# Softmax sums as a row through HBM in place of columns: one change to a conformer block on one Trainium2 core

## The chip, the cores and the metric

The kernel runs on one core of a Trainium2 chip. A core has a matmul engine (TensorE, "PE" in the profile; its weight loads are listed apart as "PEld"), a vector engine (VectorE, "DVE"), a scalar engine (ScalarE, "ACT"), GpSimd ("POOL") and a sync engine ("SP") that only issues transfers here. The metric is device time in microseconds (us). "Span" is the time from the first to the last instruction in a profile of one execution. The "granted clock" is the share of TensorE's full clock that the profile shows as granted (1.00 is full, 0.50 half).

## The reference, cut to what matters

The reference is a conformer block in bf16, for 2 batches of 4000 tokens of 512 features: feed-forward, attention, convolution, feed-forward, each with a layer norm and a residual. The change touches the attention:

```python
q = h @ w_q
k = h @ w_k
v = h @ w_v
scores = jnp.einsum('btd,bsd->bts', q, k) * scale
p = _softmax(scores, axis=-1)
attn = jnp.einsum('bts,bsd->btd', p, v) @ w_o
x2 = x1 + attn
```

## The kernel before

The queries are worked on in 16 chunks of 500. For one chunk the kernel goes through 32 tiles of keys. For each tile TensorE computes scores for 128 keys (125 used) by 500 queries, ScalarE takes the exponential into a tile `P`, VectorE adds `P` to a running sum `acc` (keys on the partitions), and four tiles later TensorE multiplies the values with `P` into four banks `Yb` of PSUM (the buffers that TensorE's results go to). The division by the softmax sum comes last, when the output projection is added to the residual: there the sum must lie with queries on the partitions, as `rl` of 125 x 4. When the last values of a chunk are done, this runs:

```python
def finish_queries(self, b, qc, done):
    S, s = self.S, qc % 2
    for dc in range(DC):                      # the output copies: two on VectorE, two on ScalarE
        if dc % 2:
            S.op("DVE", lambda e, dc=dc: e.tensor_copy(self.OT[:, dc, :], self.Yb[dc][:, 0:CHUNK]), ...)
        else:
            self.act(self.OT[:, dc, :], self.Yb[dc][:, 0:CHUNK], AF.Copy, ...)
    S.op("DVE", lambda e: e.tensor_copy(self.ahi, self.acc[s]), ...)              # the splits
    S.op("DVE", lambda e: e.tensor_tensor(out=self.alo, in0=self.acc[s], in1=self.ahi, op=ALU.subtract), ...)

    def sums():
        ps, b_ps = self.sbank()
        for ti in range(TPC):                 # 4 x 2 matmuls of one column
            for part, bp in ((self.ahi, self.b_ahi), (self.alo, self.b_alo)):
                self.mm(ps[0:TILE, ti:ti + 1], part[:, ti * TILE:(ti + 1) * TILE], self.onec[:, 0:1], ...)
        S.op("DVE", lambda e: e.reciprocal(self.rl[s], ps[0:TILE, 0:TPC]), ...)
    ...
    self.after(1 if last else 2, sums)        # so many tiles later
    for ti in range(TPC):
        self.after((2 if last else 4) + ti, lambda ti=ti: project(ti))
```

The comments are added and the read and write lists are cut. The values lag the scores by four tiles, so all this falls into the fourth tile of the next chunk. The program writes down the instructions of each engine in one order; a recording layer puts a semaphore wait (for a signal of another engine) ahead of each instruction that needs one. The scores, the sums and the projections take turns on four PSUM banks. The place between two chunks is called a boundary below. Its cost is the time by which the scores behind it start later than they would if the scores and values of the two chunks followed each other without a gap.

Of the kernel before, what the change touches and what calls it, by code (L numbers as in the profile page):

```python
# [5 lines left out]
F32 = mybir.dt.float32  # L6
BF16 = mybir.dt.bfloat16
I32 = mybir.dt.int32
ALU = mybir.AluOpType
AF = mybir.ActivationFunctionType  # L10
# [3 lines left out]
TILE = 125  # L14
CHUNK = 500
TPC = CHUNK // TILE
# [4 lines left out]
TB = T // TILE  # L21
# [197 lines left out]
class Conformer:  # L219
# [15 lines left out]
    def memory(self):  # L235
        nc = self.nc
# [35 lines left out]
        C = Region(nc, "work", 48992)  # L272
        off = [0]

        def take(n):
            o = off[0]
            off[0] += n
            return o

        oLT = take(2 * 4096)  # L280
# [69 lines left out]
        def small(n, dt=F32, parts=128):  # L350
            return C.view(take(n * (2 if dt == BF16 else 4) + 3 & ~3), n, dt, parts)
# [37 lines left out]
        self.b_one3 = Buf("one3")  # L389
        self.m3 = C.view(oLT + 4096, CHUNK, parts=3)  # L390
        self.b_m3 = [C.buf("m3", oLT + 4096 + j * 250, 250) for j in range(TPC)]
        self.mx = small(TCB, parts=TILE)
        self.b_mx = [Buf("mx") for _ in range(TCB)]
        self.mc = [small(1, parts=TILE) for _ in range(3)]
# [247 lines left out]
    def attention(self, old, hook, done):  # L642
        S = self.S
        LAG = 4
        for g in range(NCK):
            b, qc = divmod(g, TCB)
            s = qc % 2
            if self.any_score:
                if qc == 0:
                    self.pop(len(self.lags))  # L650
                    if b:
                        for kt in range(TB):
                            self.second_keys(kt)
                        for dc in range(DC):
                            self.q_group(1, 0, dc)
                self.row_max(qc)
            for kt in range(TB):
                kc, kj = divmod(kt, TPC)
                ps, b_ps = self.sbank()
                p = self.nxt("P", self.NP)  # L660
                for cc in range(DC):
                    self.mm(ps[:, 0:CHUNK], self.hT[kc][:, kj, cc, :], self.qT[s][:, cc, :],
                            cc == 0, cc == DC - 1 and not self.any_score,
                            [self.b_hT[kc][kj], self.b_qT[s][cc]], b_ps)
                if self.any_score:
                    self.mm(ps[:, 0:CHUNK], self.one3, self.m3, False, True,
                            [self.b_one3] + self.b_m3, b_ps)
                self.act(self.P[p], ps[:, 0:CHUNK], AF.Exp, [b_ps], [self.b_P[p]], scale=SCALE)
                if kt == 0:
                    S.op("DVE", lambda e, p=p: e.tensor_copy(self.acc[s], self.P[p]),  # L670
                         reads=[self.b_P[p]], writes=[self.b_acc[s]])
                else:
                    S.op("DVE", lambda e, p=p: e.tensor_tensor(  # L673
                        out=self.acc[s], in0=self.acc[s], in1=self.P[p], op=ALU.add),
                        reads=[self.b_P[p], self.b_acc[s]], writes=[self.b_acc[s]])

                def values(kt=kt, p=p, b=b, qc=qc):
                    for dc in range(DC):
                        self.mm(self.Yb[dc][:, 0:CHUNK], self.h[kt][:, dc * 128:(dc + 1) * 128], self.P[p],
                                kt == 0, kt == TB - 1, [self.b_h[kt], self.b_P[p]], self.b_Y[dc],  # L680
                                inc=kt == TB - 1 or dc == DC - 1)
                    if kt == TB - 1:
                        self.finish_queries(b, qc, done)

                self.lags.append(values)
                if g == 0 and kt < LAG:
                    self.pop({0: old // 2, 1: old - old // 2}.get(kt, 0))
                elif len(self.lags) > LAG:
                    self.pop(1)
                if g + 1 < NCK and kt in (14, 16, 18, 20) and not (self.any_score and g + 1 == TCB):  # L690
                    self.q_group((g + 1) // TCB, (g + 1) % TCB, (kt - 14) // 2)
                if not self.any_score:
                    if g == TCB - 1 and kt >= 6:
                        self.second_keys(kt - 6)
                    if g == TCB and kt < 6:
                        self.second_keys(TB - 6 + kt)
                hook(g, kt)
                self.tick()

    def second_keys(self, kt):  # L700
# [3 lines left out]
        self.load(self.h[kt], src, [self.b_h[kt]], reads=[self.b_keys2[kc]])  # L704
        self.transpose(self.hT[kc][:, kj], src, [self.b_keys2[kc]], [self.b_hT[kc][kj]])

    def finish_queries(self, b, qc, done):
        S, s = self.S, qc % 2
        for dc in range(DC):
            if dc % 2:  # L710
                S.op("DVE", lambda e, dc=dc: e.tensor_copy(self.OT[:, dc, :], self.Yb[dc][:, 0:CHUNK]),  # L711
                     reads=[self.b_Y[dc]], writes=[self.b_OT[dc]])
            else:
                self.act(self.OT[:, dc, :], self.Yb[dc][:, 0:CHUNK], AF.Copy, [self.b_Y[dc]], [self.b_OT[dc]])
        S.op("DVE", lambda e: e.tensor_copy(self.ahi, self.acc[s]), reads=[self.b_acc[s]], writes=[self.b_ahi])  # L715
        S.op("DVE", lambda e: e.tensor_tensor(out=self.alo, in0=self.acc[s], in1=self.ahi, op=ALU.subtract),  # L716
             reads=[self.b_acc[s], self.b_ahi], writes=[self.b_alo])

        def sums():
            ps, b_ps = self.sbank()  # L720
            for ti in range(TPC):
                for part, bp in ((self.ahi, self.b_ahi), (self.alo, self.b_alo)):
                    self.mm(ps[0:TILE, ti:ti + 1], part[:, ti * TILE:(ti + 1) * TILE], self.onec[:, 0:1],
                            part is self.ahi, part is self.alo, [bp, self.b_onec], b_ps,
                            inc=part is self.alo and ti == TPC - 1)
            S.op("DVE", lambda e: e.reciprocal(self.rl[s], ps[0:TILE, 0:TPC]),
                 reads=[b_ps], writes=[self.b_rl[s]])

        def project(ti):
            ps, b_ps = self.sbank()  # L730
            for dc in range(DC):
                self.mm(ps[0:TILE, :], self.OT[:, dc, ti * TILE:(ti + 1) * TILE], self.Wvo[:, dc, :],
                        dc == 0, dc == DC - 1, [self.b_OT[dc], self.b_Wvo], b_ps)
            self.residual(ps[0:TILE, :], b_ps, (b * TCB + qc) * TPC + ti, self.rl[s][:, ti:ti + 1],
                          [self.b_rl[s]])
            if ti == TPC - 1:
                done(b * TCB + qc)

        last = b * TCB + qc == NCK - 1
        self.after(1 if last else 2, sums)  # L740
        for ti in range(TPC):
            self.after((2 if last else 4) + ti, lambda ti=ti: project(ti))


    def conv_b(self, t, jj):
# [405 lines left out]
```

## Time and profile before

| | before |
|---|---|
| time, median of 3 runs | 2134.14 us (2133.32 to 2136.76) |
| span of the profiled run | 2132.2 us |
| busy: PE, DVE, ACT | 97%, 51%, 34% |
| share of the chain that ended last: PE, DVE | 93%, 3% |
| period of one chunk in attention | 69.42 us |

The chain is followed back from the last instruction; an engine's share in it is the part of the span in which the end waited for that engine. The period is the distance between the first one-column matmuls of two neighbouring chunks; in the trace 13 of the 15 distances are within 0.01 us of 69.42 (the first and the last chunk do less work beside attention). The lines themselves are shown in the prediction.

### The profile page before, as it was taken

What the parts mean: (1) busy time and instruction counts of PE and PEld (TensorE: products, weight loads), DVE (VectorE), ACT (ScalarE), POOL (GpSimd) and SP (SyncE); (2) the same over time, 40 slices, a digit from 0 to 9 for tenths busy, and PEclk for the clock granted to TensorE, in tenths of its full rate; (3) what the DMA queues carried; (4) which work ended last, traced back from release to release, by engine and by line L of the source; (5) the groups of instructions that cost most, each with busy time, mean ns of one, the idle gap of its engine ahead of it and who ended that gap; (6) DMA issues with size and microseconds to landing.
All of it is one profiled execution on the core that took longest, in us unless ns stands there. A gap on an engine that the chain in (4) does not pass through costs nothing.

```text
span 2132.2 us, 24365 instructions
## 1 busy us (share of the span) xinstructions
PE 2058.9 (97%) x9674; PEld 1038.7 (49%) x9674; DVE 1090.5 (51%) x2229; ACT 732.7 (34%) x1248; POOL 122.9 (6%) x257
## 2 busy tenths in 40 slices
PE   4999999999999999999999999999987999999996
PEld 2555555554444444444444444444444555555553
DVE  2444433335555666656665666566745434444442
ACT  1433333333333333333333333333324433443332
POOL 0111100000000000000000000000000000000000
PEclk9999999999999999999999999999999999999998
DMA  7122222110000000004300000000233011111110
GB/s 177 34 56 59 59 60 59 49 49 11 11 5 13 18 15 20 8 18 114 80 10 18 15 18 13 15 18 16 59 107 99 21 38 35 35 30 40 40 38 23
DMA packets 199327, 85.39 MB, mean 40 GB/s; under 512 B 147873, under 2 KB 198692, under 8 KB 199204
## 3 DMA queue, kind: packets, MB, share of 16 engines
q1 hardware_dynamic: 186468, 75.35, 14.6%
q10 hardware_dynamic: 12736, 8.39, 1.5%
q8 instruction: 78, 1.28, 0.3%
q14 instruction: 45, 0.37, 0.1%
HBM read 29.53 MB, written 19.04 MB: 23 GB/s over the span
## 4 chain that ended last, share of the span: by engine, by line
PE 93%; DVE 3%; issue 1%; DMA 1%; ACT 0%; SPq 0%; POOL 0%; ACTq 0%; POOLq 0%; DVEq 0%
PE s L453 53%; PE y L453 39%; DVE work L711 1%; DVE work L716 1%; DVE work L673 0%; DMA xt<-in_x_dram 0%; ACT work L457 0%; DVE work L491 0%; SPq L465 0%; DMA work<-work 0%; DVE work L715 0%; DVE work L514 0%; POOL work L501 0%; DVE xt L560 0%; ACTq L461 0%
## 5 line engine op out<-in xcount | busy, mean ns | idle before, releaser
L457 ACT ACTIVATE work<-s 128x500 bf16<-128x500 f32 (+1 forms) x1068 | 626.8, 587 | 1266.6 <-PE s L453 1262.0
L453 PE MATMUL s<-work,wff 128*128 128x500 bf16 x2560 | 634.3, 378 | 32.2 <-DMA work<-work 28.8
L453 PE MATMUL y<-work,keys 128*128 128x500 bf16 x2048 | 519.1, 374 | 1.3
L453 PE MATMUL s<-work,keys 128*128 128x500 bf16 x2048 | 517.5, 374 | 0.1
L453 PE MATMUL y<-wff,work 128*125 128x512 bf16 x2048 | 514.8, 379 | 0.0
L673 DVE TENSOR_TENSOR work<-work 128x500 f32<-128x500 f32 x496 | 334.8, 675 | 304.6 <-ACT work L457 302.9
L453 PEld LDWEIGHTS s<-work,wff 128*128 128x128 bf16 x2560 | 251.1, 98 | 313.3 <-issue 33.7
L453 PEld LDWEIGHTS y<-wff,work 128*125 128x125 bf16 x2048 | 279.6, 137 | 176.4
L453 PEld LDWEIGHTS y<-work,keys 128*128 128x128 bf16 x2048 | 198.0, 97 | 244.4 <-DVE work L711 15.6
L453 PEld LDWEIGHTS s<-work,keys 128*128 128x128 bf16 x2048 | 199.2, 98 | 228.9 <-DVE work L602 0.6
L560 DVE SCALAR_TENSOR_TENSOR xt<-y,xt 125x512 bf16<-125x512 f32 x128 | 79.4, 683 | 385.5 <-PE y L453 385.5
L491 DVE BATCH_NORM_STATS2 work<-xt 125x6 f32<-125x512 bf16 x320 | 201.6, 679 | 16.8 <-DMA xt<-in_x_dram 16.8
L453 PE MATMUL s<-work 128*125 128x512 bf16 (+2 forms) x646 | 144.8, 347 | 20.8 <-DVE work L716 7.9
L501 POOL TENSOR_TENSOR work<-work 125x4 f32<-125x4 f32 x80 | 85.5, 1068 | 1189.2 <-DVE work L499 1189.2
L514 DVE TENSOR_SCALAR work<-xt,work 125x512 bf16<-125x512 bf16 x288 | 116.0, 449 | 20.1 <-POOL work L501 20.1
L453 PEld LDWEIGHTS s<-work 128*125 128x125 bf16 (+1 forms) x646 | 81.1, 139 | 72.1 <-issue 10.8
L560 DVE SCALAR_TENSOR_TENSOR xt<-s,xt 125x512 bf16<-125x512 f32 x64 | 43.8, 691 | 134.4 <-PE s L453 134.4
L755 DVE SCALAR_TENSOR_TENSOR wff<-wff,s 128x500 bf16<-128x500 f32 x64 | 43.2, 676 | 63.7 <-PE s L453 63.7
L457 ACT ACTIVATE wff<-s 128x500 f32<-128x500 f32 x64 | 37.6, 587 | 81.3 <-PE s L453 76.8
L560 DVE SCALAR_TENSOR_TENSOR xt<-s,work,xt 125x512 bf16<-125x512 f32 x64 | 48.0, 750 | 34.0 <-PE s L453 33.1
L453 PE MATMUL s<-keys,work 128*128 128x500 bf16 x256 | 64.4, 376 | 0.0
L457 ACT ACTIVATE work<-keys,work 128x500 bf16<-128x500 bf16 x64 | 49.6, 794 | 5.9 <-DMA wff<-in_w_ff_a_dram 4.0
(51 smaller groups left out, 397.7 us busy)
## 6 DMA issues: line engine op xcount, KB each, us to landing
xt<-in_x_dram SPq DMA_DIRECT2D x15, 500.0 KB
out_dram<-work SPq DMA_DIRECT2D x15, 500.0 KB
dcvd<-wff SPq DMA_DIRECT2D x52, 125.0 KB, 1.7
keys<-dcvd SPq DMA_DIRECT2D x13, 500.0 KB
wff<-in_w_ff_a_dram ACTq DMA_DIRECT2D x16, 256.0 KB
keys<-work SPq DMA_DIRECT2D x8, 512.0 KB, 3.5
keys<-keys SPq DMA_DIRECT2D x32, 128.0 KB
work<-work SPq DMA_TRANSPOSE x192, 2.5
```

The source lines that it names most:

```text
L453: self.S.op("PE", lambda e: e.matmul(out, lhsT, rhs, start=start, stop=stop), reads=reads, writes=[bank], inc=stop if inc is None else inc)
L457: return self.S.op("ACT", lambda e: e.activation(out, in_, func, **kw), reads=reads, writes=writes)
L491: self.S.op("DVE", lambda e: e.bn_stats(self.st[sl][:, ti, :], self.XT[g]), reads=[self.bx[g]], writes=[self.b_st[sl][ti]])
L501: S.op("POOL", lambda e: e.tensor_tensor(out=self.rs[sl], in0=self.va[sl], in1=self.neghalf[0:TILE, :], op=ALU.pow), reads=[self.b_va[sl], ...
L514: self.S.op("DVE", lambda e: e.tensor_scalar(out, self.XT[g], self.mv[sl][:, ti, 0:1], self.rs[sl][:, ti:ti + 1], ALU.subtract, ALU.mult), ...
L560: self.S.op("DVE", lambda e: e.scalar_tensor_tensor(out=self.XT[g], in0=ps, scalar=scalar, in1=self.XT[g], op0=ALU.mult, op1=ALU.add), rea ...
L673: S.op("DVE", lambda e, p=p: e.tensor_tensor(out=self.acc[s], in0=self.acc[s], in1=self.P[p], op=ALU.add), reads=[self.b_P[p], self.b_acc[ ...
L711: S.op("DVE", lambda e, dc=dc: e.tensor_copy(self.OT[:, dc, :], self.Yb[dc][:, 0:CHUNK]), reads=[self.b_Y[dc]], writes=[self.b_OT[dc]])
L716: S.op("DVE", lambda e: e.tensor_tensor(out=self.alo, in0=self.acc[s], in1=self.ahi, op=ALU.subtract), reads=[self.b_acc[s], self.b_ahi], ...
L755: self.S.op("DVE", lambda e: e.scalar_tensor_tensor(out=self.G[gs][:, jj, 1:1 + CHUNK], in0=self.th[k], scalar=1.0, in1=ps[:, 0:CHUNK], op ...
```

## The change

The intent is to have fewer matmuls on TensorE: two 500-column matmuls with a ones column as weights give all 500 sums as one row. The row lies on one partition, so it is stored to HBM (the memory outside the core) and loaded back with the queries on the partitions. The splits move to the last score tile, and the projections come two tiles later. The last chunk keeps the columns.

```diff
+                if kt == TB - 1:
+                    self.split_sums(s)
...
-        S.op("DVE", lambda e: e.tensor_copy(self.ahi, self.acc[s]), ...)
-        S.op("DVE", lambda e: e.tensor_tensor(out=self.alo, in0=self.acc[s], in1=self.ahi, op=ALU.subtract), ...)
+        def sum_row():
+            ps, b_ps = self.sbank()
+            for part, bp in ((self.ahi, self.b_ahi), (self.alo, self.b_alo)):
+                self.mm(ps[0:1, 0:CHUNK], self.onec[:, 0:1], part, part is self.ahi, part is self.alo,
+                        [bp, self.b_onec], b_ps)
+            self.act(self.row, ps[0:1, 0:CHUNK], AF.Copy, [b_ps], [self.b_row])
+            self.store(self.rowd[s:s + 1, :], self.row, [self.b_row], [self.b_rowd[s]])
+            k = S.dsems[self.nxt("ld", 12)]
+            S.dma("SP", k, lambda e: e.dma_start(self.sq[s], self.rowd[s].rearrange("(t p) -> p t", p=TILE),
+                                                 allow_slow_non_contiguous=True), ...)
...
-        self.after(1 if last else 2, sums)
+        if last:
+            self.after(1, sums)
+        else:
+            sum_row()
+            self.after(5, lambda: S.op("DVE", lambda e: e.reciprocal(self.rl[s], self.sq[s]), ...))
         for ti in range(TPC):
-            self.after((2 if last else 4) + ti, lambda ti=ti: project(ti))
+            self.after((2 if last else 6) + ti, lambda ti=ti: project(ti))
```

The new buffers and the two moved lines inside `split_sums` are cut.

More of the change, by code (lines that the diff above doesn't have):

```diff
@@ L391, in memory @@
         self.b_m3 = [C.buf("m3", oLT + 4096 + j * 250, 250) for j in range(TPC)]
+        self.row = C.view(oLT + 6144, CHUNK, F32, parts=1)
+        self.b_row = C.buf("row", oLT + 6144, 2000)
+        self.sq = [small(TPC, parts=TILE) for _ in range(2)]
+        self.b_sq = [Buf("sq") for _ in range(2)]
+        self.rowd = nc.dram_tensor("rowd", [2, CHUNK], F32, kind="Internal").ap()
+        self.b_rowd = [Buf("rowd") for _ in range(2)]
         self.mx = small(TCB, parts=TILE)
@@ L705, in second_keys, with split_sums @@
         self.transpose(self.hT[kc][:, kj], src, [self.b_keys2[kc]], [self.b_hT[kc][kj]])
+    def split_sums(self, s):
+        S = self.S
+        S.op("DVE", lambda e: e.tensor_copy(self.ahi, self.acc[s]), reads=[self.b_acc[s]], writes=[self.b_ahi])
+        S.op("DVE", lambda e: e.tensor_tensor(out=self.alo, in0=self.acc[s], in1=self.ahi, op=ALU.subtract),
+             reads=[self.b_acc[s], self.b_ahi], writes=[self.b_alo])
     def finish_queries(self, b, qc, done):
@@ L714, in finish_queries @@
                 self.act(self.OT[:, dc, :], self.Yb[dc][:, 0:CHUNK], AF.Copy, [self.b_Y[dc]], [self.b_OT[dc]])
-        S.op("DVE", lambda e: e.tensor_copy(self.ahi, self.acc[s]), reads=[self.b_acc[s]], writes=[self.b_ahi])
-        S.op("DVE", lambda e: e.tensor_tensor(out=self.alo, in0=self.acc[s], in1=self.ahi, op=ALU.subtract),
-             reads=[self.b_acc[s], self.b_ahi], writes=[self.b_alo])
+        def sum_row():
[7 more added lines that the diff above has]
+            S.dma("SP", k, lambda e: e.dma_start(self.sq[s], self.rowd[s].rearrange("(t p) -> p t", p=TILE),
+                                                 allow_slow_non_contiguous=True),
+                  reads=[self.b_rowd[s]], writes=[self.b_sq[s]])
         def sums():
@@ L739, in finish_queries @@
         last = b * TCB + qc == NCK - 1
-        self.after(1 if last else 2, sums)
+        if last:
+            self.after(1, sums)
+        else:
+            sum_row()
+            self.after(5, lambda: S.op("DVE", lambda e: e.reciprocal(self.rl[s], self.sq[s]),
+                                       reads=[self.b_sq[s]], writes=[self.b_rl[s]]))
         for ti in range(TPC):
-            self.after((2 if last else 4) + ti, lambda ti=ti: project(ti))
+            self.after((2 if last else 6) + ti, lambda ti=ti: project(ti))
     def conv_b(self, t, jj):
```

## The prediction

> **What bounds the kernel now.** I read the page in this order: the busy table, the granted clock, the chain, then single chunk boundaries in the timeline of each engine.
>
> ```profile
> PE 2058.9 (97%) x9674; PEld 1038.7 (49%) x9674; DVE 1090.5 (51%) x2229; ACT 732.7 (34%) x1248; POOL 122.9 (6%) x257
> ...
> PE 93%; DVE 3%; issue 1%; DMA 1%; ACT 0%; SPq 0%; POOL 0%; ACTq 0%; POOLq 0%; DVEq 0%
> PE s L453 53%; PE y L453 39%; DVE work L711 1%; DVE work L716 1%; DVE work L673 0%; DMA xt<-in_x_dram 0%; ACT work L457 0%; DVE work L491 0%; SPq L465 0%; DMA work<-work 0%; DVE work L715 0%; DVE work L514 0%; POOL work L501 0%; DVE xt L560 0%; ACTq L461 0%
> ```
>
> TensorE (PE) carries the end; VectorE (DVE) and ScalarE (ACT) are half idle or more. Only what removes TensorE instructions or TensorE waits is worth anything. The chain names the lines the change touches: L711 copies the attention output out of PSUM, L715 and L716 split the softmax sums into a high and a low bf16 part. Together they are a little over 1% of the span. They recur once per query chunk, of which there are 16. Here is one boundary on TensorE (columns: start us, length us, operation, count, idle before it and its releaser):
>
> ```profile
> 609.30 1.00 PE L453 MATMUL y<-work,keys 128*128 128x500 bf16 x4
> 610.14 1.01 PE L453 MATMUL s<-work,keys 128*128 128x500 bf16 x4
> 610.99 1.42 PE L453 MATMUL y<-work,keys 128*128 128x500 bf16 x4
> 612.36 0.22 PE L453 MATMUL s<-work 128*125 128x1 bf16 x1
> 613.07 0.56 PE L453 MATMUL s<-work 128*125 128x1 bf16 x7 [0.49 <-DVE work L716]
> 613.49 1.01 PE L453 MATMUL s<-work,keys 128*128 128x500 bf16 x4
> ```
>
> The first row is the last value product of the old chunk. Then come scores, the first value product of the new chunk, the eight one-column matmuls, and scores again. In steady state four 500-column matmuls advance TensorE by 0.845 us (609.30 to 610.14, 610.14 to 610.99), so the scores at 613.49 would start at 610.14 + 2 x 0.845 = 611.83 with nothing between. The boundary costs 1.66 us, in three parts: the value product is stretched by 612.36 - 611.83 = 0.53; the first one-column matmul and the wait behind it take 613.07 - 612.36 = 0.71; the other seven take 613.49 - 613.07 = 0.42, or 60 ns each. I read the same timeline at all fifteen inner boundaries: fourteen cost 1.66 within 0.01, the first 1.72. The reasons are in the weight loads and in VectorE:
>
> ```profile
> 611.44 0.11 PEld L453 LDWEIGHTS y<-work,keys 128*128 128x128 bf16 x2 [0.56 <-DVE work L711]
> 612.03 0.10 PEld L453 LDWEIGHTS y<-work,keys 128*128 128x128 bf16 x1 [0.47 <-DVE work L711]
> ...
> 610.12 0.68 DVE L673 TENSOR_TENSOR work<-work 128x500 f32<-128x500 f32 x1 [1.01 <-ACT work L457]
> 610.72 1.26 DVE L711 CAST work<-y 128x500 bf16<-128x500 f32 x2
> 611.89 0.41 DVE L715 CAST work<-work 128x500 bf16<-128x500 f32 x1
> 612.34 0.68 DVE L716 TENSOR_TENSOR work<-work 128x500 bf16<-128x500 f32 x1
> ```
>
> VectorE does a running sum, two output copies, then both splits, back to back, and TensorE waits for each in turn. But the split input was ready four score tiles earlier: the values lag the scores by four tiles.
>
> The sixteenth boundary is worse:
>
> ```profile
> 1571.01 1.01 PE L453 MATMUL y<-work,keys 128*128 128x500 bf16 x4
> 1573.52 0.22 PE L453 MATMUL s<-work 128*125 128x1 bf16 x1 [1.50 <-DVE work L715]
> 1574.23 0.91 PE L453 MATMUL s<-work 128*125 128x1 bf16 x7 [0.50 <-DVE work L716]
> 1575.00 1.83 PE L453 MATMUL s<-work,wff 128*128 128x500 bf16 x4
> 1576.62 4.12 PE L453 MATMUL s<-work 128*125 128x512 bf16 x16
> ```
>
> **What the Trainium skill says.** "TensorE: Matmul & The Clock Gate", Back-to-back issue gap: a warm matmul takes N/2.4 + 2.5 ns and below 64 columns there is a floor of about 60 cycles. For 500 columns that is 211 ns; the trace has 0.845/4 = 211, so it agrees. For one column the trace has 60 ns, above the floor's 25: each here also loads a 125-column weight. "DMA: Bandwidth & Descriptors", Anatomy of one DMA: about 2.0 us fixed per transfer. The trace agrees nearly: a 125 KB store to HBM lands in 1.7 us (median of 52). Same page, Rules for kernel authors: a non-contiguous last dimension "lowers to one descriptor per element". The new load writes 125 partitions x 4 separate floats, so 500 pieces of 4 bytes. Same page, Why a DMA increments its semaphore by 16 and not by 1: the number of engines is the largest up to 16 that divides the slowest dimension, so 5 for 125, or 100 pieces each. Nothing in the trace of before shows such a load.
>
> **The change part by part.** (1) *Splits moved* from the end of the values to just after the last score tile's sum. VectorE does the same 0.41 + 0.68 us, four tiles earlier, where a tile lasts 1.69 us and the running sum takes 0.68 of it. The splits no longer stand in the boundary; the 0.49 us wait on L716 and the one on L715 should vanish. (2) *Eight one-column matmuls removed* at 15 boundaries: with (1) they and their waits were 0.71 + 0.42 = 1.13 us. (3) *Two 500-column matmuls added* with the ones column as weights, at once after the last values: 2 x 0.211 = 0.42 us. They stand before the scores, so they also delay the first value product by 0.42, and VectorE gets that time for its copies: the stretch of 0.53 shrinks to about 0.11. New boundary: 0.42 + 0.11 = 0.53. Saved: 1.66 - 0.53 = 1.13 us, times 15 = 17.0 us (17.1 with the costlier first).
>
> (4) *The last boundary* keeps its eight matmuls, but its splits are done long before. TensorE can begin them at about 1572.0 in place of 1573.5, and ends them 0.5 later; one group of four matmuls follows, then the projections, which need the copies (at the latest 1573.14 in the chain). So the projections may start near 1573.4 to 1574 in place of 1576.62. In before the group from 1575.00 takes 1.62 us for four matmuls, twice the usual, so TensorE seems slow after its wait; I can't tell whether this stays. The chain runs through here into the last chunk's normalization. I take 3 us, out of 2 to 4.
>
> (5) *Round trip through HBM*, 15 times. One ACT copy of the 1x500 row, which I estimate at the 587 ns that 128x500 copies take, behind the two output copies: done some 1.8 us after the last values. Store 1.7 us plus 0.3 of issue; then the load: 0.6 issue, 2 fixed, and 100 pieces per engine at 26 ns (the share of queue 1, 14.6% of 16 x 2132 us over 186468 packets, gives 27 ns) makes 2.7. Estimated arrival: about 9 us after the last values. The reciprocal is queued on VectorE behind the running sum of the fifth tile iteration, nominally about 7.7 us (9.4 with convolution work in between) after the values. So VectorE may stand for a microsecond. That costs TensorE nothing: the projections come one tile later, and the first stall could come only when the third projection needs the bank of the first, at about 15 us. Nothing at the end of the span: the last chunk uses no round trip.
>
> (6) *Projections, and the normalization behind them, two tiles (about 4 us) later.* Their transposes end near tile 20; the convolution reads them at tile 22. Free.
>
> Sum: 17 + 3 = 20 us; 2134.1 - 20 = 2114 us, 0.9% less.
>
> **The rivals.** *The output copies bind.* If VectorE is later than I think (its 1.09 us of splits now falls beside the convolution taps' work of tiles 29 to 31), the value product keeps its whole 0.53: saved 0.71 x 15 + 2 = 13 us, so 2121. For: the same engine ends both waits. Against: the splits are four tiles away, and the waits of VectorE on ACT (0.7 to 1.4 us before most running sums) show room. *The round trip binds.* If a 4-byte piece costs 100 ns or more in place of 26, the load takes 13 us; the reciprocal then holds the VectorE queue, and with it residuals, banks and TensorE: a few us in 15 chunks, so 2125 to 2180. Against: the slack of 15 us. *The Sync queue blocks.* It now waits for the row, then for its store, and other transfers stand behind. Beside it run second-batch keys from 963 to 1036 us, back to back; the row of the eighth chunk queues there. For: the queue is full. Against: it is one chunk, and those keys are read about 24 tiles later. Costs 0 to 5 us once. *Only the matmul count matters*: 8 x 60 ns out, 422 ns in, that is nothing: 2133. Against: the waits are in the chain.
>
> **Range and chances.** 2109 if the last boundary gives 4 and the value stretch vanishes (1.24 x 15 = 18.6) and a little more; 2121 from the first rival. Two percent faster would be 2091, more than every wait at every boundary together (16 x 1.7 = 27 would only reach 2107): 1%. Slower by 2% needs the second rival in full: 2%. Within: 97%.
>
> **What would show it.** Right: 9584 matmuls (9674 - 90); no wait of TensorE on the split lines at inner boundaries; a chunk period 1.13 us shorter than the 69.4 us of before (617.04 to 686.46); a value product of about 1.1 in place of 1.42 us; a row load landing in under 6 us. Wrong: VectorE idle for many us before the reciprocal, TensorE waiting for residuals or transposes at tiles 8 to 22, or a value product as long as before.

## The result, and the profile after

The changed kernel took 2118.46 us (median of 4 runs, 2117.57 to 2120.55) beside 2133.73 us of the kernel before (median with a fourth run). The ratio is 0.9927, with a 95% interval of 0.991 to 0.9945. Ratios here are the mean time of one kernel's fast runs over that of the other's of the same rounds, so not quite the ratio of the medians. The gain is 15.3 us by the medians, or about 15.6 by the ratio; the prediction was 20, and 2118.46 lies within its range of 2109 to 2121.

The busy table and the chain of the changed kernel:

```profile
PE 2050.4 (97%) x9582; PEld 1032.4 (49%) x9584; DVE 1090.0 (52%) x2229; ACT 739.3 (35%) x1263; POOL 118.7 (6%) x257
...
PE 95%; issue 1%; DVE 1%; DMA 1%; SPq 0%; POOL 0%; ACT 0%; POOLq 0%; ACTq 0%; DVEq 0%
```

There are 9584 weight loads, 90 fewer, as predicted (two matmul records are missing from the trace). VectorE's share of the chain fell from 3% to 1%. VectorE's work is unchanged, so only its place has changed. The same boundary as in the prediction, TensorE and then its weight loads, in the timeline of the changed kernel (the line numbers of the kernels differ; L453 and L460 are the helper that issues every matmul):

```profile
607.72 1.00 PE L460 MATMUL y<-work,keys 128*128 128x500 bf16 x4
608.66 0.58 PE L460 MATMUL s<-work 128*1 128x500 bf16 x2
609.17 1.02 PE L460 MATMUL s<-work,keys 128*128 128x500 bf16 x4
610.03 1.00 PE L460 MATMUL y<-work,keys 128*128 128x500 bf16 x4
610.87 1.01 PE L460 MATMUL s<-work,keys 128*128 128x500 bf16 x4
...
608.66 0.09 PEld L460 LDWEIGHTS s<-work 128*1 128x1 bf16 x2 [0.41 <-ACT work L464]
609.17 0.54 PEld L460 LDWEIGHTS s<-work,keys 128*128 128x128 bf16 x4 [0.43 <-issue]
```

Without anything between, the scores at 610.87 would start 3 x 0.845 us after 607.72, at 610.255. The boundary costs 0.61 us in place of 1.66, and the chunk period is 68.38 in place of 69.42. The value product is not stretched at all (1.00, from 1.42). The row matmuls themselves cost more than their 0.42: they start 0.10 us after the values could have ended (608.66 against 608.565), and the scores come 0.51 after them. In both places the weight load begins together with its matmul, where weight loads elsewhere begin 0.2 us ahead.

On VectorE the splits are gone from behind the copies, and the reciprocal comes 9.7 us after the last values (618.22 - 608.565) without a wait of its own:

```profile
609.14 1.26 DVE L728 CAST work<-y 128x500 bf16<-128x500 f32 x2
...
618.22 0.17 DVE L770 RECIPROCAL work<-work 125x4 f32<-125x4 f32 x1
```

The round trip on the sync engine's queue, of the same boundary:

```profile
609.93 0.23 SPq L476 DMA_DIRECT2D rowd<-work  x1
611.06 0.25 SPq L741 DMA_DIRECT2D work<-rowd  x1
```

The load is issued when the store has landed, so the store took 1.13 us from issue. The load's pieces moved from 611.94 to 612.67. VectorE never waits for a transfer in the attention stage of this trace. The last boundary of the changed kernel:

```profile
1554.90 1.01 PE L460 MATMUL y<-work,keys 128*128 128x500 bf16 x4
1555.74 0.57 PE L460 MATMUL s<-work 128*125 128x1 bf16 x8
...
1557.02 3.62 PE L460 MATMUL s<-work 128*125 128x512 bf16 x16
```

The projections start 2.12 us after the last value product's start, where it was 5.61 (1571.01 to 1576.62). Both waits of this boundary are gone.

### The profile page after: what moved, and what is told of

It is laid out like the page before. It is cut to its first block, busy times and chain, and to the rows that moved or that the text cites. A ratio compares the mean times of both kernels' runs of the same rounds, so it can differ in the third digit from the quotient of the medians.

```text
span 2113.7 us, 24196 instructions
## 1 busy us (share of the span) xinstructions
PE 2050.4 (97%) x9582; PEld 1032.4 (49%) x9584; DVE 1090.0 (52%) x2229; ACT 739.3 (35%) x1263; POOL 118.7 (6%) x257
## 4 chain that ended last, share of the span: by engine, by line
PE 95%; issue 1%; DVE 1%; DMA 1%; SPq 0%; POOL 0%; ACT 0%; POOLq 0%; ACTq 0%; DVEq 0%
PE s L460 54%; PE y L460 41%; DMA xt<-in_x_dram 0%; DVE work L498 0%; SPq L472 0%; DMA work<-work 0%; DVE work L521 0%; POOL work L508 0%; DVE xt L567 0%; DMA wff<-in_w_ff_b_dram 0%; DMA wff<-in_w_ff_a_dram 0%; DVE wff L851 0%; DVE wff L786 0%; DVE work L504 0%; SPq L468 0%
## 5 line engine op out<-in xcount | busy, mean ns | idle before, releaser
L464 ACT ACTIVATE work<-s 128x500 bf16<-128x500 f32 (+1 forms) x1083 | 635.3, 587 | 1244.0 <-PE s L460 1242.7
L460 PE MATMUL s<-work,wff 128*128 128x500 bf16 x2560 | 630.9, 377 | 32.3 <-DMA work<-work 28.9
L460 PE MATMUL s<-work,keys 128*128 128x500 bf16 x2048 | 517.6, 374 | 0.1
L460 PE MATMUL y<-wff,work 128*125 128x512 bf16 x2048 | 514.8, 379 | 0.0
L460 PE MATMUL y<-work,keys 128*128 128x500 bf16 x2048 | 514.0, 373 | 0.0
L460 PEld LDWEIGHTS s<-work,wff 128*128 128x128 bf16 x2560 | 250.8, 98 | 313.3 <-issue 32.5
L460 PEld LDWEIGHTS y<-wff,work 128*125 128x125 bf16 x2048 | 279.6, 137 | 176.4
L460 PEld LDWEIGHTS y<-work,keys 128*128 128x128 bf16 x2048 | 199.2, 97 | 234.0 <-DVE xt L567 0.2
L460 PEld LDWEIGHTS s<-work,keys 128*128 128x128 bf16 x2048 | 198.6, 98 | 234.9 <-issue 6.0
L460 PE MATMUL s<-work 128*125 128x512 bf16 (+2 forms) x556 | 140.7, 377 | 12.2 <-ACT work L464 8.8
L508 POOL TENSOR_TENSOR work<-work 125x4 f32<-125x4 f32 x80 | 81.1, 1014 | 1240.0 <-DVE work L506 1240.0
L460 PEld LDWEIGHTS s<-work 128*125 128x125 bf16 (+1 forms) x556 | 72.5, 134 | 64.1 <-ACT work L464 11.5
L460 PE MATMUL s<-keys,work 128*128 128x500 bf16 x256 | 64.4, 376 | 0.0
L567 DVE SCALAR_TENSOR_TENSOR xt<-s,work,xt 125x512 bf16<-125x512 f32 x64 | 47.9, 749 | 16.0 <-PE s L460 15.7
```

The source lines that it names most:

```text
L460: self.S.op("PE", lambda e: e.matmul(out, lhsT, rhs, start=start, stop=stop), reads=reads, writes=[bank], inc=stop if inc is None else inc)
L464: return self.S.op("ACT", lambda e: e.activation(out, in_, func, **kw), reads=reads, writes=writes)
L508: S.op("POOL", lambda e: e.tensor_tensor(out=self.rs[sl], in0=self.va[sl], in1=self.neghalf[0:TILE, :], op=ALU.pow), reads=[self.b_va[sl], ...
L567: self.S.op("DVE", lambda e: e.scalar_tensor_tensor(out=self.XT[g], in0=ps, scalar=scalar, in1=self.XT[g], op0=ALU.mult, op1=ALU.add), rea ...
```

## The experiments

The first question was which part of the change gains. Theory M says it is the moved splits; rival R says it is the row.

**split_only**: the kernel before, with the splits moved.

```diff
+                if kt == TB - 1:
+                    self.split_sums(s)
...
-        S.op("DVE", ... self.ahi ...)      # in finish_queries
-        S.op("DVE", ... self.alo ...)
```

> The kernel before with one part of the change: the two splits moved to the last score tile; the eight one-column matmuls stay where they were, after the first value product of the new chunk. Theory M (the gain is the moved splits; the row and HBM only replace cheap matmuls): a boundary loses the waits for the splits but keeps the value product stretched by 0.53 us and pays 8 x 60 ns = 0.48, so about 1.0 in place of 1.66 us: 0.65 x 15 = 10 us, plus 4 us at the last boundary, less some 2 us that the stretch after attention gave back in the changed kernel: 12 us, ratio 0.9945. Rival R (the row and its way round are the gain): nothing at the inner boundaries, 2 us at the last: 0.999.

Measured: 2121.43 us, ratio 0.9934 (0.9922 to 0.9946), chunk period 68.61. The move alone is most of the gain: 0.81 of the 1.04 us of the period, and 0.66 of the 0.73% of the time. It did better than expected; TensorE at the boundary shows why:

```profile
607.74 1.01 PE L453 MATMUL s<-work,keys 128*128 128x500 bf16 x4
608.59 1.42 PE L453 MATMUL y<-work,keys 128*128 128x500 bf16 x4
609.85 0.57 PE L453 MATMUL s<-work 128*125 128x1 bf16 x8
610.28 1.01 PE L453 MATMUL s<-work,keys 128*128 128x500 bf16 x4
```

The boundary is 610.28 - 607.74 - 1.69 = 0.85: 0.43 for the eight columns and 0.42 for the stretch, where I had read 0.53. The other 0.11 in the kernel before was the start of the first one-column matmul, which waited for a split.

**cols_at_once**: the columns also issued at once after the values.

```diff
-        self.after(1 if last else 2, sums)
+        if last:
+            self.after(1, sums)
+        else:
+            sums()
```

> As split_only, and the eight one-column matmuls issued at once after the last values, where the changed kernel issues its row; no row, no HBM, projections where they were. Theory M: the eight matmuls (0.48 us) fill the time that the value product would wait for the copies, so a boundary costs 0.53 to 0.61 us, as with the row (0.61): as fast as the changed kernel or up to 1 us faster, ratio to before 0.992 to 0.993. Rival R: clearly slower than the changed kernel, 0.997 or more.

Measured: 2112.07 us, ratio 0.989 (0.9874 to 0.9906), period 68.20. This kernel has neither row nor HBM and beats the changed kernel, by more than expected. Its boundary:

```profile
606.73 1.01 PE L453 MATMUL y<-work,keys 128*128 128x500 bf16 x4
607.57 0.57 PE L453 MATMUL s<-work 128*125 128x1 bf16 x8
608.00 1.01 PE L453 MATMUL s<-work,keys 128*128 128x500 bf16 x4
608.85 1.00 PE L453 MATMUL y<-work,keys 128*128 128x500 bf16 x4
```

Eight one-column matmuls take 0.43 us (607.57 to 608.00), as much as two of 500 columns should. They hold the value product back by that time, so that VectorE's running sum and copies get far enough ahead, and the product comes unstretched. There is no gap ahead of the columns or behind them. Of the 6.4 us between the medians of the two kernels the boundaries are 2.7 (0.18 x 15); 1.2 is time outside the span, and 1.9 lies behind attention (46.91 us in this profile against 48.84), both taken up below.

**row_only**: the changed kernel with the splits back in their old place, and the row two tiles later.

```diff
-                if kt == TB - 1:
-                    self.split_sums(s)
...
+        self.split_sums(s)                 # behind the output copies
...
-            sum_row()
+            self.after(2, sum_row)
```

> The changed kernel with the splits back behind the output copies, and the two row matmuls two tiles later, where the columns were; round trip, reciprocal and projections as changed. Theory M: the waits for the splits are back (0.53 stretch, 0.71 for the first matmul with its wait), and the second row matmul takes 0.21 in place of 0.42: a boundary of about 1.5 us, last boundary as before: gain 0 to 3 us, ratio 0.9985 to 1.000. Rival R: it keeps most of the gain, 0.994.

Measured: 2134.53 us, ratio 0.9999 (0.9986 to 1.0012), period 69.31. The wait for the split is back:

```profile
612.35 0.37 PE L460 MATMUL s<-work 128*1 128x500 bf16 x1 [0.34 <-DVE work L718]
```

The row and the round trip by themselves gain 0.1 us a chunk, which the time does not show. Rival R falls.

**before_again**: the kernel before, unchanged.

> The kernel before once more, against itself: ratio 1.000 within 0.001. It is run for the relation between time and span: the changed kernel gained 18.5 us of span in the two profiles but 15.3 us of time between medians. If the span of a usual run of before is near 2129.5 (its profiled run was 2.3 us slower than the median), the two agree and nothing is lost outside the span; if it is 2132 with a time of 2133.5, the changed kernel loses about 3 us outside its span.

Measured: 2135.34 us, ratio 0.9999. Five of its six runs lay between 2133.19 and 2137.21, and one at 2138.49; the spans went from 2129.2 to 2134.7. The profiled run that the prediction was made from was thus at the slow end. Time minus span was 3.7 to 4.1 us in all runs of before, against 4.85 to 5.07 in the four of the changed kernel.

The second question was what the row's extra 0.19 us is, and whether the round trip is as far off the path as predicted.

**after_again**: the changed kernel, unchanged.

> The changed kernel once more. Its ratio should be 0.9927 within 0.001. Two things about it are open: its time lay 5.0 us above its span in all four runs, that of the six other kernels' runs 3.7 to 4.1; if this comes from the kernel, 5.0 returns here, if from the chip or the launch, 3.9 and a ratio near 0.992. And TensorE waited 8.8 us for ScalarE near the last weight loads, against 7.4 to 7.9 in the kernels with columns at every boundary; row_only, which has rows, had 8.9: if the rows cause it, 8.8 again.

Measured: 2120.16 us, ratio 0.9926; time minus span 4.7 to 5.4 us. So the extra 1.2 us outside the span belongs to the kernel. The wait of TensorE for ScalarE was 8.7 us again; but later profiles of kernels with columns had 8.2 (cols_again) and 8.4 (hi_copies_first), and ones128 with rows had 7.7, so the rows do not explain it.

**one_wait**: both row matmuls declared to need both splits.

```diff
-                        [bp, self.b_onec], b_ps)
+                        [self.b_ahi, self.b_alo, self.b_onec], b_ps)
```

> The changed kernel with both row matmuls declared to need both splits, so that the second needs no wait of its own. In the changed kernel a boundary costs 0.61 us where two 500-column matmuls are 0.42; TensorE starts the row 0.10 late and the scores 0.09 late. Theory W (the semaphore waits keep the weight loads from being issued ahead): part of the 0.19 goes, boundary 0.52 or less, 1.4 us faster in all. Rival C (loading weights of one column does not overlap with the matmul before and after it): 0.61 as before. For C: the columns at once have the same waits and no such gap.

Measured: 2118.83 us, ratio 0.9927, period 68.38. Nothing changed, so theory W gets no support. It isn't refuted by this run alone: only the second matmul lost its wait, the first kept one. The next run keeps both.

**ones128**: ones in 128 columns as the weights.

```diff
-                self.mm(ps[0:1, 0:CHUNK], self.onec[:, 0:1], part, ...)
+                self.mm(ps[:, 0:CHUNK], self.ones, part, ...)       # ones: 128 x 128, rows 0 to 124 are 1
```

> The changed kernel with a ones matrix of 128 columns as the row's weights in place of one column (all 128 output rows are then the same sum; row 0 is used). Same waits. Theory W: boundary 0.61, as in the changed kernel. Rival C: the weights load ahead like all others and the boundary is 0.42 to 0.45, some 2.7 us faster in all, ratio about 0.9915.

Measured: 2114.59 us, ratio 0.9907 (0.9892 to 0.9922), period 68.19. TensorE and the weight loads:

```profile
607.80 0.58 PE L462 MATMUL s<-work 128*128 128x500 bf16 x2
608.23 1.01 PE L462 MATMUL s<-work,keys 128*128 128x500 bf16 x4
...
607.60 0.31 PEld L462 LDWEIGHTS s<-work 128*128 128x128 bf16 x2
```

The weight loads run ahead again by 0.2 us, and the boundary is 0.43. More weights are faster than fewer: the gap came with the one-column weights. Both waits are still there, so theory W falls. So does the wait for ScalarE that the profile names before the row's weights in the changed kernel: here they load at 607.60, before the last exponential ends at 607.75. That confirms rival C as to the cause being the weights (with them go the rows of the result, 1 against 128, which can't be changed apart); why one column does not load ahead is not shown.

**hops3**: three more round trips ahead of the last.

```diff
-            self.store(self.rowd[s:s + 1, :], self.row, [self.b_row], [self.b_rowd[s]])
+            for hop in range(4):
+                self.store(self.rowd[s:s + 1, :], self.row, [self.b_row], [self.b_rowd[s]])
+                if hop < 3:
+                    self.load(self.row, self.rowd[s:s + 1, :], [self.b_row], reads=[self.b_rowd[s]])
```

> The changed kernel with three more round trips through HBM ahead of the last (row stored, loaded back, stored again). The changed kernel's load had its packets done about 4.5 us after the last values, and the reciprocal came on VectorE at 9.7 us. A hop should take 2.5 to 3.5 us, so the sums arrive at 12 to 15 us. My theory that the round trip lies off the path with some 15 us of room: VectorE now waits a few us at the reciprocal, TensorE does not, time as the changed kernel within 1 us. Rival (any wait of VectorE passes on to TensorE): 2 to 5 us at each of 15 boundaries, 30 to 75 us slower.

Measured: 2115.91 us, ratio 0.992. VectorE waited 39.8 us in all at the 15 reciprocals (6.5 at most), TensorE 1.6 us at one boundary. The reciprocal at the boundary shown above:

```profile
619.57 0.18 DVE L773 RECIPROCAL work<-work 125x4 f32<-125x4 f32 x1 [2.32 <-DMA work<-rowd]
```

A wait of VectorE of this length, in this place, is free. This kernel is even some us faster than after_again of the same chip; 1.2 of that is time outside the span (3.8 us here), and the rest is within the scatter of single spans (2111.6 to 2115.0 here, 2110.8 to 2116.1 there).

**hops6**: the same with six (`range(7)`, `hop < 6`).

> As hops3, with six more round trips. hops3 showed 2.6 us a hop and the reciprocal 12.05 us after the last values, with VectorE waiting 2.3 us and TensorE not. Six put the reciprocal at 12.05 + 7.8 = 19.9 us after the values. By my account TensorE's first stall comes where the third projection needs the bank of the first, 15.9 us after the values; the first residual would then be done at about 21.3, so TensorE stalls some 5.5 us at each of 15 boundaries: 80 us slower than the changed kernel (40 to 110), ratio 1.03. Rival (the room is larger, or the stall is made up): within 10 us of the changed kernel.

Measured: 2229.46 us, ratio 1.0449 (1.0431 to 1.0467), some 110 us slower than the changed kernel, at the upper end of what was expected. TensorE and VectorE at the same boundary:

```profile
637.79 1.97 PE L460 MATMUL s<-work 128*125 128x512 bf16 x4 [5.17 <-DVE xt L567]
...
636.31 0.18 DVE L773 RECIPROCAL work<-work 125x4 f32<-125x4 f32 x1 [10.00 <-DMA work<-rowd]
```

The matmuls at 637.79 are the third projection: the stall is where the prediction put it, and of the size expected (5.17 against 5.5). TensorE waited 83.4 us for residuals in all, 3.4 of them in a place behind attention where before waits as well, so 80 at the boundaries, as expected. The rest is a second cost that I had left out: after the wait the granted clock was 0.50 for 3.3 us (637.79 to 641.10), so eight matmuls took twice their time, some 1.7 us at this stall. Over all 15 stalls the clock records show 68 us at 0.50, which costs up to 34 us.

The third question was whether a better version is to be had.

**cols_hi_only**: cols_at_once with the sums from the high part alone, so four matmuls and one split.

```diff
-        S.op("DVE", ... self.alo ...)
...
-                for part, bp in ((self.ahi, self.b_ahi), (self.alo, self.b_alo)):
-                    self.mm(ps[0:TILE, ti:ti + 1], part[:, ti * TILE:(ti + 1) * TILE], self.onec[:, 0:1], ...)
+                self.mm(ps[0:TILE, ti:ti + 1], self.ahi[:, ti * TILE:(ti + 1) * TILE], self.onec[:, 0:1], ...)
```

> cols_at_once with the sums taken from the high bf16 part alone: four one-column matmuls in place of eight, no second split. It gives slightly less exact denominators (one bf16 rounding per partition, averaged over 125 partitions). With four matmuls between the values and the scores VectorE's copies have 0.22 us less time. If the value product needs the 0.53 us I took from before, the boundary stays at 0.43 or so and nothing is gained; if the copies have room, the boundary falls towards 0.22, up to 3 us faster than cols_at_once, ratio 0.9877.

Measured: 2115.17 us, ratio 0.9912 (0.9896 to 0.9929), period 68.18, correct. The columns now take 0.20 us, but the value product is stretched again:

```profile
606.29 1.00 PE L453 MATMUL y<-work,keys 128*128 128x500 bf16 x4
...
608.18 1.22 PE L453 MATMUL y<-work,keys 128*128 128x500 bf16 x4
609.25 1.01 PE L453 MATMUL s<-work,keys 128*128 128x500 bf16 x4
...
608.43 0.11 PEld L453 LDWEIGHTS y<-work,keys 128*128 128x128 bf16 x2 [0.36 <-DVE work L718]
...
607.11 0.68 DVE L673 TENSOR_TENSOR work<-work 128x500 f32<-128x500 f32 x1 [1.01 <-ACT work L457]
607.71 1.25 DVE L718 CAST work<-y 128x500 bf16<-128x500 f32 x2
```

The boundary is 609.25 - 606.29 - 3 x 0.845 = 0.42. The product's weights wait for the copies (L718), so 0.42 us is a floor as long as VectorE's work stands in this order: running sum, then copies.

**hi_copies_first**: the same, with the running sum of the fourth tile issued behind the output copies.

```diff
+                late = g > 0 and kt == LAG - 1
+                if not late:
+                    add()                  # the running sum of this tile, as before
...
                 elif len(self.lags) > LAG:
                     self.pop(1)            # here the copies are issued
+                if late:
+                    add()
```

> cols_hi_only with VectorE's output copies issued ahead of the running sum of the fourth tile, which stood before them. cols_hi_only showed a boundary of 0.42 us in place of cols_at_once's 0.43: what four matmuls saved, the value product waited for the copies (1.22 us in place of 1.00). If the copies are the floor, taking 0.6 us from in front of them lets the boundary fall to the four matmuls, 0.20 to 0.25 us: 3 us faster than cols_at_once. If something else holds it, 0.42 as before.

Measured: 2110.87 us, ratio 0.9889 (0.9873 to 0.9906), period 67.96. The floor was the running sum in front of the copies: they now start at 607.43, right behind the values, and the sum comes after them. The boundary is 609.54 - 606.81 - 2.535 = 0.20:

```profile
606.81 1.00 PE L453 MATMUL y<-work,keys 128*128 128x500 bf16 x4
...
609.54 1.01 PE L453 MATMUL s<-work,keys 128*128 128x500 bf16 x4
...
607.43 1.26 DVE L725 CAST work<-y 128x500 bf16<-128x500 f32 x2 [0.81 <-PE y L453]
```

The period says 0.24 x 15 = 3.6 us less than cols_at_once. The medians of the shared rounds differ by 1.5 us (2112.40 for cols_again) and the intervals overlap, so the time alone does not prove it; the period does for the stage.

**cols_again**: cols_at_once, unchanged.

> cols_at_once once more, as the yardstick on the same chip and for its spread: its first four runs lay within 0.8 us, those of every other kernel spread over 3 to 5. Ratio 0.989 to 0.991.

Measured: 2112.40 us (2111.38 to 2114.86), ratio 0.9899 (0.9882 to 0.9915). The lead over the changed kernel holds; the narrow spread of its first runs was luck.

## Why the prediction was right, and where its terms were off

Its main reading holds: the waits for the splits were the gain, the round trip is hidden, and TensorE was the only thing to count. The runs confirm each of these apart (split_only 0.9934, row_only 0.9999, hops3 0.992). The sum was 4 to 5 us too good, from several terms. One reading of the chain was off without harm: L711, L715 and L716 are 0.9%, 0.3% and 0.5% of it, so 1.7% and not "a little over 1%".

1. *Splits moved.* Right. There is no wait of TensorE on the split lines in the changed kernel.
2. *Eight matmuls and their waits out, 1.13 us.* Right in the sum, but the split into parts was misread: the stretch is 0.42, and 0.11 of "0.53" belonged to the first one-column matmul.
3. *Two matmuls in, 0.42, plus 0.11 of stretch.* The step is mis-sized. No stretch remained, but the one-column weights cost 0.19 of gaps, so 0.61 in place of 0.53 (ones128: 0.43). Over 15 boundaries the gain was 1.04 to 1.05, so 15.7 us in place of 17.1.
4. *Last boundary, 3 us out of 2 to 4.* Right, as far as two profiles can tell. From the last run of 16 value products to the end of the projections the changed kernel took 10.64 us (1549.83 to 1560.47). Before took 14.64 (1565.94 to 1580.58) and in the repeat 13.02, so the gain was 2.4 to 4.0. The difference between the two runs of before is the clock: in the first it was 0.50 from 1574.2 to 1576.6, after a wait, which is the slowness that the prediction noted and could not place.
5. *Round trip.* Right that it is free, too pessimistic in its size: the load's pieces had moved by about 4.1 us after the values, not 9. The pieces took 9 ns each and not 26 (507 packets from 610.0 to 612.9 made 9.8% of 16 engines' 2.9 us). Of the 507 two belong to the store; the load's 505 are the predicted 500 and five more, one for each engine if five took part, as predicted (the profile doesn't tell the engines apart). The 2.0 us was misapplied: the page's section, "Anatomy of one DMA — SWDGE (gpsimd) path", is about transfers that GpSimd issues, and these are issued by the sync engine. Here the load's first piece moved 0.88 us after its issue and the last was done after 1.61. The limit was as worked out: hops3 below it, hops6 above it, with the stall at the third projection.
6. *Projections later.* Right. No wait for them or for the transposes appears.

Two losses were not in the sum at all. Time outside the span grew by 1.2 us: 5.0 in the changed kernel, one_wait and ones128, and 3.7 to 4.1 in all others, row_only and hops3 among them. It follows the kernel and not the chip, but what makes it stays open. And the stretch behind attention gave some back. From the end of the last projections to the second group of 32 matmuls of the next stage, the changed kernel took 48.84 us and in the repeat 48.36, before 46.83 and 47.34. In the changed kernel 4.3 us of this ran at a granted clock of 0.55 (1569.3 to 1573.6) and the 1.86 us ahead of it at 0.50, behind a wait of 3.40 us that before has too. "TensorE: Matmul & The Clock Gate", What's actually happening, says that the clock halves after an idle window of about 3.4 us and that the window runs freely. The traces fit the free-running window: in the clock records of all runs each stretch between two changes is a whole number of 3.41 us, and with the same 3.40 us wait cols_at_once still had 0.96 just behind it and 0.50 only from 1.1 us later. But the window need not be idle throughout: in before the clock halved at 1574.2 after 3.41 us in which TensorE had been busy for 1.44. So the phase has a part in what a wait costs: behind the same 3.40 us wait the clock stayed at 0.50 for 5.7 us in the changed kernel and for 2.7 in its repeat. This explains the first profile of the changed kernel only; the 48.36 of the repeat has another cause, which stays open. hops3, with the same rows, took 46.36 us for the stretch; so I don't count this as caused by the change.

15.7 for the boundaries, about 3 for the last, less 1.2 outside and 1 to 2 behind attention, makes 15.5 to 16.5; the ratio says 15.6. That is no close check, since the last boundary and the stretch behind attention each vary by 1 to 2 us from profile to profile.

Of the rivals, "the output copies bind" was half right: with the running sum in front of them they do set a floor, at 0.42 us, which the row's matmuls just cover (cols_hi_only, hi_copies_first). "The Sync queue blocks" did happen, without cost: behind the chunk whose row met the keys (row at 1018.96) the store was issued 2.96 us after the row and the load 5.65, where 1.27 and 2.40 are usual; the reciprocal at 1028.52 did not wait, and the period stayed 68.38. "The round trip binds" came true only in hops6. "Only the matmul count matters" missed that the moved splits come with the row.

## What to carry to other kernels

When an idea changes an operation and moves its inputs earlier in the same edit, try the move alone: here it held most of the gain, and the old operation in the new place cost 0.43 us a boundary where the new one cost 0.61 (and 0.43 only with padded weights). Work that must sit on the busiest engine is cheapest where that engine would wait anyway, so place it by the gap and not by its count. Here the detour off the path cost nothing until it met the first buffer that had to come free; look for that buffer and its time, and it tells how long the detour may be.

## What the Trainium skill lacked or had wrong

- "TensorE: Matmul & The Clock Gate", LDWEIGHTS (loading the stationary operand), has the load time follow the number of columns. It does not say that weights of one column are not loaded ahead: a boundary with two such loads cost 0.61 us, with 128 columns 0.43, while 125 columns (cols_at_once) load ahead as well.
- "DMA: Bandwidth & Descriptors" has a fixed cost of a whole transfer for the GpSimd path, none for transfers that the sync engine issues. Here a 2 KB row to HBM let the next transfer be issued 1.13 us after its own issue, and its plain load back 1.48 us after (hops3, 610.00 to 611.48). No page has a figure for pieces of 4 bytes: 9 ns each here.
- No page says why the time outside the span differs between kernels as alike as these ("Runtime: NRT & Kernel Launch" would be the place): 3.7 to 4.1 us in most kernels here and 4.7 to 5.4 in three, reproducibly by kernel.
